# Packed attention and a gated convolution on one core: keys and queries turned by VectorE, scores in 32x32 tiles, the convolution moved to TensorE

## The chip, the cores and the metric

The kernel runs on one core of a Trainium2 chip. The metric is the device time of one execution in microseconds (us); lower is better. The kernel before took 320.68 us, the median of three runs (319.39 to 321.31). The core has TensorE (PE: matmuls and the transposes that go through its array; PEld is its weight load), VectorE (DVE), ScalarE (ACT), GpSimd (POOL) and SyncE (SP), which issues all DMA transfers here. Matmul results land in PSUM, which has eight banks of 512 f32 columns on 128 partitions.

## The reference

There are 8 batches, 8 heads, 576 tokens, 64 features a head and 32 packed rows `p` a head. The first attention lets the packed rows look at the tokens; the second lets the tokens look at the packed result. Its output, laid side by side over the heads (`x`, 576 x 512 a batch), goes through a causal convolution of five taps for each feature, a sigmoid, and two 512 x 512 weights:

```python
p_packed = softmax(p @ k^T / 8) @ v            # 32 x 64 for each head
x = softmax(q @ p_packed^T / 8) @ p_packed     # 576 x 64 for each head
gate_pre = sum(conv_w[j] * shift(x, 4 - j) for j in range(5))
out = (sigmoid(gate_pre) * (x @ w_val)) @ w_out
```

Everything is f32; the three weights arrive in double precision, and the kernel rebuilds f32 values from their 32-bit words.

## The kernel before, in words

All work of a batch is cut into streams with a letter each: loads `K`, `V`, `Q`, `P`; `k` and `q` (turning keys and queries so that the features lie on the partitions), `a` (first attention), `p` (turning the packed result), `s` (second scores and their exponentials), `t` (the normalised weights, split in a high and a low part), `w` (packed result times `w_val`), `x` (the attention output itself), `g` (convolution and gate), `v` (value product times gate), `o` (output product), and for the weights `L`, `W`, `C`, `O`. The string `ORDER` is a list of steps (`a1.2`: two steps of stream `a` of batch 1) written out ahead of the run. `InOrder` (line 82) makes each engine issue its instructions exactly in the order in which `ORDER` makes them. An instruction that waits therefore holds up all that stand behind it on its engine. The bar in `ORDER` closes the pool in which the raw weights lie, and opens the one for `gvh` and `gvl`.

What the steps do, for each batch:

- `load` (line 191) brings k, v and q as two tiles each of 96 partitions, four heads to a tile.
- `transposed` (line 296) turns one tile by 12 PE transposes of 96 x 96 into a PSUM bank, in three groups of four, and ACT copies each group to `kT` or `qT`. So k and q take 48 transposes and 12 copies a batch.
- `scores` (line 309) makes 8 matmuls for four heads, each with 64 contraction rows and 32 output partitions, 288 columns: the eight 64 x 32 tiles of the array. A batch has two for the first attention and two for the second.
- `attn_pack` (line 334) takes maximum (DVE), exponential (ACT), turns the weights by 6 PE transposes for each four heads (`at`, `a1t`), and multiplies by v (`pv`, 24 matmuls of 96 x 32).
- `attn_out` (line 384) turns the second scores by DVE's 32 x 32 transpose (`t2`), takes the maximum over 32 (DVE), subtracts it (POOL), takes the exponential (ACT); `weighted` sums (DVE), multiplies by the reciprocal (POOL), turns back (DVE, `a2`) and splits into `a2h` (ACT) and `a2l` (DVE).
- `mixed` (line 451) computes x itself: four groups of four matmuls with tiles of 32 x 64 (`x`), copied by ACT to `xp`.
- `gate` (line 483) makes the convolution from `xp`: one ACT multiplication and four DVE multiply-adds for each of four chunks of 128 features, then a tanh on ACT that stands for the sigmoid.
- `value` (line 503) makes 4 chunks of 12 matmuls (three products of high and low parts); DVE multiplies by the gate, ACT and DVE split the result into `gvh` and `gvl`.
- `project` (line 556) makes the output in 9 chunks of 128 tokens for each two batches, 12 matmuls of 512 columns a chunk (`o`).

PSUM is cut into two buffers of two banks (`big`), three of one bank (`mid`) and one of one bank (`out`) for the output product.

A product in f32 shows in the profile as two MATMUL records and one in fp32r, or a PE transpose, as one.

Of the kernel before, what the change touches and what calls it, by code (L numbers as in the profile page):

```python
# [45 lines left out]
ORDER = """
x0 L0.5 P0 W0.2 K0 W0 K0 W0 Q0 W0 P1 W0.3 V0 L0 W0 V0 Q0 W0.5 C0 L0 k0 W0 k0 P2 C0 W0 C0 W0 k0 C0 W0 C0 k0.4 K1
W0 C0 L0 k0.2 W0 k0.2 C0 W0 a0 k0 C0 W0 k0 a0 k0 K1 q0 W0 a0.2 W0 k1 q0.2 a0 k1 P3 q0.2 a0.3 L0 a0.2 Q1 a0 q0
a0.3 O0 V1 a0.7 O0 a0 O0 a0 O0.2 a0 p0 V1 O0.2 p0 O0 s0 O0 q0 w0 s0 q0 O0 s0 q0 O0 w0 s0 O0 w0 s0 q0.2 Q1 O0 t0
k1 q0 s0 k1 O0 k1 t0 s0 k1.2 K2 O0 k1 a1 t0 O0.2 s0 t0 x0 a1 O0 s0 k1 t0 a1 O0 k1.2 s0 k1.2 K2 t0 x0.2 k1 k2 P4  # L50
O0 x0 a1 O0 t0 g0 a1 q1 O0 g0 x0 a1.3 k2 g0 q1.2 a1.2 t0 q1.2 a1.2 g0 Q2 t0 x0 a1 O0 a1 q1 g0 x0.2 O0 a1 V2 g0
t0 v0 x0 O0 a1 g0 O0.2 a1 g0 q1 a1.2 O0 v0 a1.2 O0 a1 q1 g0 a1 O0.3 k2 O0 a1 p1 V2 k2.2 p1 q1 k2.2 q1 s1 g0 k2
K3 k2 O0 a2 k2 s1 k2 O0 q1 k2 a2 k2 O0.2 Q2 w1 s1 K3 q1 O0 g0 q2 s1 a2 g0 w1 O0 s1.3 w1 k2 k3 P5 O0 g0 q2.2 s1
a2 q2 x1 g0 q2 s1 | v0 a2 k3 Q3 q2 k3 v0 a2 v0 k3 s1 a2 g0 k3 a2 t1 q2 k3 a2.2 q2.2 a2 g0 a2 t1 q2 k3 v0 a2.2 k3
K4 g0 v0 k3 q2 a2 V3 k3.2 t1 Q3 g0 a2.2 g0 x1 v0 t1 g0 v0 q2 x1 t1 a2 t1 k3 x1 a2 k3 g0 t1 a2.2 x1 K4 v0 a2.2 k3
g0 v0 k4 V3 a2 a3 P6 p2 t1 p2 a3 t1 s2 v0 a3 q3 g0 q3 v0 s2 g0 x1 t1 g1 x1 v0 g1 v0 a3 x1 s2 k4 x1 g1 s2 a3 q3
k4 x1 g1 a3 q3.2 Q4 a3 w2 g1 s2 q3 v0 o0 g1 t2 g1 w2 g1 t2 k4 w2 v1 o0 g1 o0 t2 o0 g1 t2 v1 g1 v1 t2 s2 g1 x2.2
v1 g1 o0 g1 q3 a3 k4 x2 o0 s2 o0 a3 q3 g1 k4 s2 g1 s2 v1 g1 o0.2 s2 o0 v1 g1.2 t2 v1 g1 t2 a3 v1 o0 v1 a3 o0 x2
g1 a3 k4 t2 a3.2 k4 K5 v1 x2 q3 g1 a3 k4 V4 v1 a3.3 g1 k4 q3 v1.2 x2 g1 a3 q3 g2 v1 k4 a3 Q4 x2 q3 g2 v1 a3 g2
a3.2 x2 v1 x2 k4 V4 a3 g2 k4 t2 o1 K5 k4 t2 x2 g2.3 v2 o1 g2 o1 g2 a4 v2 p3 o1 p3 a4 v2 g2 a4 v2 g2 s3 o1 x3 w3  # L60
g2 o1 s3 g2 q4 s3 v2 w3 g2 s3 q4 w3 q4 o1 q4 v2 s3 g2 v2 t3 s3 o1 g2 t3 a4 o1 s3 q4 k5 o1 a4 q4 Q5 k5 g2 P7 a4.2
g2 s3 g2 t3 s3 a4 o1 k5 g2 x3 a4 o1 s3 a4 o1 t3 v2 a4 g2 x3 k5 t3 g2 v2 t3 o1.2 g2 t3 x3 v2 g2 a4 k5 a4.2 v2 t3
k5.2 v2 a4 v2 V5 k5 K6 a4 t3 x3.2 t3 a4 k5 g3 v2 x3 a4 k5 g3 k5 v2 a4 q4 g3 a4 q4 v2 o2 k5 x3 g3.2 a4 g3 x3 a4
g3 a4 x3 g3 q4 v3 V5 a4 q4 g3 o2 g3 o2.2 v3 g3 v3.2 g3 x4 g3 p4 q4 o2 g3 k5 p4 Q5 a5 k5 g3 o2 s4 q4 K6 o2 a5 s4
a5 g3 s4 g3 s4 a5 o2 w4 g3 o2 a5 g3 q5 a5.3 g3 o2 a5 g3 s4 w4 g3 q5 t4 a5 o2 s4 w4 a5 t4 k6 o2 a5 q5 k6 a5 s4 a5
q5 t4 v3 a5 V6 s4 t4 g3 s4 x4 v3 g3 q5 t4 k6 v3 Q6 s4 v3.2 q5 k6 t4 k6 x4 q5 k6.2 v3 q5 x4 t4 K7 k6 a5 v3 a5 q5
k6 t4 x4.2 q5 v3.2 t4 g4 t4 x4 a5 g4 k6 a5 k6 a5 v3 a5 x4 q5 g4 a5 x4 Q6 q5 v3 g4 k6 v3 o3 x4 g4.3 a5 o3 g4 k6
a5 a6 V6 k6 g4 o3 k7 p5 g4 o3 p5 K7 a6 g4 a6 g4 x5 a6 g4 s5 o3 g4 k7.2 o3 a6 q6 k7.2 g4 q6 o3 a6.2 s5 k7 g4 s5
v4 o3 g4 s5 o3 g4 q6 g4 v4 a6 w5 s5 g4 q6 a6 s5 t5 v4 a6 q6 w5 o3 g4 t5 Q7 q6 s5 a6 g4 q6 s5 o3 a6 k7 q6 g4 s5
o3.2 a6 k7 t5 g4 w5 t5 s5 t5 x5 o3 v4 k7 o3 t5 v4 x5 k7 t5 k7 v4 x5 k7 t5 v4 a6 x5.2 v4 x5 a6 V7 a6 g5 a6 v4 a6  # L70
g5 t5 x5 g5 a6 q6 v4 a6.2 x5 q6 g5 a6 v4 a6 t5 x5 q6 g5 a6 a7 V7 q6 Q7 v4 p6 g5 v4 a7 g5 p6 g5 a7 k7 v4 s6 k7 g5
v4 a7 q7 s6 q7.2 g5 w6 q7 v4 o4 g5 w6 a7 x6 g5 s6 a7.2 s6 w6 g5 v5 o4 g5 s6 o4 g5 s6 q7 v5 a7 o4 q7 g5 a7 v5 s6
v5 s6 v5 t6 o4 s6 o4 g5 q7 a7 o4 t6 q7 a7 s6 v5 g5 v5 t6 g5 v5.2 t6 g5 o4 t6 o4 x6 t6 a7 q7 a7 o4 x6 g5 t6 q7 v5
g5 v5 x6 o4 t6 q7 o4 v5.2 t6 g5 x6 q7 t6 x6 g5 x6 g6 v5 a7 x6 g6 x6 v5 g6 a7 x6 a7.2 v5 o5 a7 g6.2 v6 o5 g6 o5
g6 a7 o5 v6 a7 g6 v6 g6 v6.2 g6 o5.2 g6 a7 o5 g6 x7 g6 v6 a7 g6 v6 g6 a7 o5 v6 o5 g6 v6 a7 g6 p7 g6 o5 g6 v6 p7
g6 v6 g6 s7 v6 o5 v6 g6 o5 s7 g6 o5 s7 g6 s7 v6.2 w7 s7 v6 o5 t7 s7 o5 o6 w7 s7 t7 w7 t7 s7 o6 x7 t7 o6 s7 o6 t7
x7 s7 t7 x7 o6 t7 o6.2 x7.2 t7 g7 t7 g7 t7 v7 o6 g7 o6 g7 x7 g7 o6 g7.2 v7 x7 g7 v7 x7 g7 o6 v7.2 o6 x7 g7.2 o7
g7.2 v7 g7 v7 g7 v7.2 o7 g7.4 v7 g7 v7.3 o7 g7.3 o7 g7 v7.3 o7.15
# [28 lines left out]
def packed_attention_gated_conv(  # L107
# [24 lines left out]

    nc = tc.nc  # L140
# [50 lines left out]
    def load(b, nm, src, order):
        for g in range(G):
            m = st[nm, b, g] = tile_of(f"{nm}m", [TP, 4, NA, 2 * D], F32, f"{nm}m_{b}_{g}")
            sp.dma_start(m, src[b, 4 * g : 4 * g + 4].rearrange(order, a=NA, c=2))
# [451 lines left out]
```

## Time and profile before

| what | value |
|---|---|
| time, median of three runs | 320.68 us |
| time, lowest and highest of the runs | 319.39 and 321.31 us |
| span of the profiled execution | 317.6 us |
| PE busy | 284.6 us (90%) |
| DVE busy | 255.0 us (80%) |
| ACT busy | 212.7 us (67%) |
| POOL busy | 67.8 us (21%) |
| bytes read and written in HBM | 33.57 and 9.44 MB |

The profile gives the span, from the first to the last instruction, of one execution; its own time outside of the span isn't given. The median of the runs is 3.1 us above that span, and this is taken as what lies around it. Almost every instruction is issued from one helper, so the profile puts nearly all at line 90, and a group is told from another by the tiles it names: `kT<-kpt` is the copy of turned keys out of PSUM, `sig<-xp,cw,sig` is one tap of the convolution. `x8` is a count of instructions. "Idle before" is the time that the engine had nothing to do ahead of the group, and behind the arrow stands what ended it.

### The profile page before, as it was taken

What the parts mean: (1) busy time and instruction counts of PE and PEld (TensorE: products, weight loads), DVE (VectorE), ACT (ScalarE), POOL (GpSimd) and SP (SyncE); (2) the same over time, 40 slices, a digit from 0 to 9 for tenths busy, and PEclk for the clock granted to TensorE, in tenths of its full rate; (3) what the DMA queues carried; (4) which work ended last, traced back from release to release, by engine and by line L of the source; (5) the groups of instructions that cost most, each with busy time, mean ns of one, the idle gap of its engine ahead of it and who ended that gap; (6) DMA issues with size and microseconds to landing.
All of it is one profiled execution on the core that took longest, in us unless ns stands there. A gap on an engine that the chain in (4) does not pass through costs nothing.

```text
span 317.6 us, 7342 instructions
## 1 busy us (share of the span) xinstructions
PE 284.6 (90%) x2996; PEld 209.2 (66%) x2996; DVE 255.0 (80%) x396; ACT 212.7 (67%) x432; POOL 67.8 (21%) x71
## 2 busy tenths in 40 slices
PE   0088786879989999999999999999999999999993
PEld 0065243747557787677786876777688788667882
DVE  0983388679999997999789986897998977878771
ACT  2247669889876768666877787777856846556422
POOL 1312572464121220132002410231023000140000
PEclk9999758899999999999999999999999999999999
DMA  7999999999973239533657558243702011111005
GB/s 165 216 219 254 262 240 223 217 229 188 233 150 107 68 102 238 138 95 97 151 128 196 166 135 199 85 116 103 152 33 66 35 42 60 54 70 45 33 0 166
DMA packets 42475, 43.48 MB, mean 137 GB/s; under 512 B 6085, under 2 KB 36805, under 8 KB 42442
## 3 DMA queue, kind: packets, MB, share of 16 engines
q1 hardware_dynamic: 42442, 43.02, 58.1%
q8 instruction: 23, 0.38, 0.6%
q14 instruction: 10, 0.08, 0.1%
HBM read 33.57 MB, written 9.44 MB: 135 GB/s over the span
## 4 chain that ended last, share of the span: by engine, by line
PE 81%; ACT 8%; DMA 5%; DVE 3%; SPq 1%; issue 1%; ACTq 0%; DVEq 0%
PE o L90 32%; PE val L90 16%; PE x L90 6%; PE s L90 6%; PE kpt L90 5%; PE qpt L90 5%; PE pv L90 3%; DMA km<-in_k_dram 3%; PE at L90 3%; PE wp L90 3%; DMA wv_words<-in_moe_w_val_dram 2%; DVE sig L90 1%; ACT a1t L90 1%; ACT a L90 1%; ACT wo_top L90 1%; SPq L90 1%
## 5 line engine op out<-in xcount | busy, mean ns | idle before, releaser
L90 DVE SCALAR_TENSOR_TENSOR sig<-xp,cw,sig 128x576 f32<-128x576 f32 x128 | 106.4, 832 | 10.8 <-ACT sig L90 9.4
L90 PE MATMUL o<-woh,gvh 128*128 128x512 f32 x144 | 59.1, 411 | 0.1
L90 PE MATMUL o<-woh,gvl 128*128 128x512 f32 x144 | 56.5, 393 | 0.0
L90 PE MATMUL o<-wol,gvh 128*128 128x512 f32 x144 | 56.4, 392 | 0.0
L90 PE MATMUL val<-a2h,wph 128*128 128x288 f32 x128 | 39.4, 308 | 0.1
L90 ACT COPY osb<-o 128x512 f32<-128x512 f32 x34 | 19.8, 584 | 27.2 <-PE o L90 18.0
L90 PE MATMUL val<-a2h,wpl 128*128 128x288 f32 x128 | 37.9, 296 | 0.0
L90 PE MATMUL val<-a2l,wph 128*128 128x288 f32 x128 | 37.7, 295 | 0.0
L90 ACT ACTIVATE sig<-sig 128x576 f32<-128x576 f32 x32 | 22.0, 688 | 18.1 <-DVE sig L90 18.0
L90 POOL TENSOR_TENSOR t<-t,mx 128x576 f32<-128x576 f32 x16 | 23.1, 1442 | 47.8 <-DVE mx L90 46.6
L90 PEld LDWEIGHTS o<-woh,gvh 128*128 128x128 f32 x144 | 27.1, 188 | 9.4 <-issue 3.0
L90 POOL TENSOR_TENSOR t<-t,rs 128x576 f32<-128x576 f32 x16 | 22.0, 1372 | 50.1 <-DVE rs L90 44.6
L90 DVE SCALAR_TENSOR_TENSOR sig<-sig,val 128x576 f32<-128x576 f32 x32 | 23.9, 748 | 10.7 <-ACT sig L90 5.4
L90 PEld LDWEIGHTS o<-woh,gvl 128*128 128x128 f32 x144 | 27.1, 188 | 6.5 <-DVE gvl L90 0.4
L90 PEld LDWEIGHTS o<-wol,gvh 128*128 128x128 f32 x144 | 27.2, 189 | 4.6
L90 ACT COPY kT<-kpt 128x384 f32<-128x384 f32 x48 | 23.3, 485 | 10.2 <-PE kpt L90 10.0
L90 PE MATMUL kpt<-ident,km 96*128 96x96 f32 x192 | 26.8, 275 | 2.5 <-DMA km<-in_k_dram 2.4
L90 PE MATMUL qpt<-ident,qm 96*128 96x96 f32 x192 | 25.7, 262 | 3.2 <-ACT pT L90 1.9
L90 PEld LDWEIGHTS qpt<-ident,qm 96*128 96x128 f32 x192 | 19.6, 147 | 13.2 <-issue 7.5
L90 ACT COPY qT<-qpt 128x384 f32<-128x384 f32 x48 | 22.9, 485 | 6.9 <-PE qpt L90 6.9
L90 DVE TENSOR_TENSOR gvl<-sig,gvh 128x576 fp32r<-128x576 f32 x32 | 25.2, 788 | 2.6 <-ACT gvh L90 2.4
L90 PEld LDWEIGHTS kpt<-ident,km 96*128 96x128 f32 x192 | 21.0, 157 | 9.2 <-issue 4.9
(77 smaller groups left out, 515.1 us busy)
## 6 DMA issues: line engine op xcount, KB each, us to landing
km<-in_k_dram SPq DMA_DIRECT2D x16, 576.0 KB, 8.2
qm<-in_q_dram SPq DMA_DIRECT2D x16, 576.0 KB, 6.7
vm<-in_v_dram SPq DMA_DIRECT2D x16, 576.0 KB, 6.7
out_dram<-osb SPq DMA_DIRECT2D x24, 256.0 KB, 2.0
wv_words<-in_moe_w_val_dram SPq DMA_DIRECT2D x8, 256.0 KB, 6.1
wo_words<-in_moe_w_out_dram SPq DMA_DIRECT2D x4, 512.0 KB, 11.0
out_dram<-osb SPq DMA_DIRECT2D x8, 192.0 KB, 2.3
p<-in_p_dram SPq DMA_DIRECT2D x16, 64.0 KB, 8.4
```

What stands on the lines that cost most here:

```text
L90: made = getattr(self.engine, op)(*args, **kw)
```

## The change

Kernel after differs in the following parts.

- k, q and v come as two tiles each of 128 partitions (`m`, nine buffers for all three). A partition holds nine tokens in a row, 2304 bytes of each of two heads. A head now lies on 64 partitions, the even heads on the lower half and the odd ones on the upper, and these halves are the two groups g.
- k, q and p are turned by one DVE instruction for each tile, in blocks of 32 x 32, into `xT` and `pT`. PE transposes and ACT copies of k and q are gone. The 64 features now lie in two blocks of 32 (`c`), one behind the other.
- The scores of a whole batch are one product into four banks (`quad`): for each of the two feature blocks 16 matmuls of 32 x 32, 288 columns, the second block added to the first in PSUM. Matmuls for a batch and attention go from 16 to 32.
- The weights of the first attention are turned by 9 full PE transposes a batch, and `pv` has 72 matmuls of 64 x 32 a batch. A DVE multiplication by the reciprocal takes the place of two on ACT.
- The attention output x isn't computed any more. POOL multiplies the packed result by each of the five taps (`taps`, stream `c`, into `ppk`), and the convolution is 5 x 8 matmuls of 32 x 64 for each half of the tokens, added in `quad`, on `a2` read at five offsets. `mixed`, its ACT copies, ACT's first tap and DVE's four are gone; the tanh reads PSUM.
- For this, `a2` has a margin of four zeros and stays in two fixed tiles, and its tokens are written with a step of nine elements.
- The tap weights are spread over partitions by 10 small matmuls with a selection matrix (`sel`) at the start.
- PSUM is now one `quad` of four banks, one `big` of two and two `mid` of one bank. The output product uses `mid`.
- `ORDER` is another list.

```diff
-PSB = {'big': 2, 'mid': 3, 'out': 1}
+PSB = {"quad": 1, "big": 1, "mid": 2}
...
-            for a in range(NA):
-                pt = one(f"{nm}pt_{b}_{g}_{a}")[:, : 4 * TP].rearrange("x (j i) -> x j i", j=4)
-                for j in range(4):
-                    pe.transpose(pt[:, j], m[:, j, a], ident[:TP, :TP])
-                yield
-                act.copy(xT[:, :, TP * a : TP * a + TP], pt)
-                yield
+            dve.transpose(
+                xT.rearrange("a h e c z -> a (h e c z)"),
+                st[nm, b, n].rearrange("a h e d -> a (h e d)"),
+            )
+            yield
...
+        for c in range(2):
+            for t in range(NQ):
+                rows = slice(NP * t, NP * t + NP)
+                for hl in range(4):
+                    pe.matmul(
+                        s[heads[hl], t].rearrange("a (e z) -> a e z", z=NP),
+                        pT(rows, c, hl),
+                        st[f"{nm}T", b, hl // 2][rows, hl % 2, :, c, :],
+                        start=(c == 0),
+                        stop=(c == 1),
+                    )
...
+            pool.tensor_tensor(
+                ppk[:, g],
+                st["ppd", b][:, g].unsqueeze(1).broadcast_to([P, NT, D]),
+                cwb[:, g],
+                op=ALU.mult,
+            )
...
+            dve.transpose(
+                a2g.rearrange("a (t z e) -> a t e z", t=2, e=NE),
+                t2.rearrange("a (t e) z -> a t e z", t=2),
+            )
...
+        for half, hc in enumerate(halves):
+            x = quad(f"gate_{b}_{half}")
+            for kk in range(NT):
+                for hl in range(4):
+                    for g in range(G):
+                        pe.matmul(
+                            x[D * g : D * g + D, hl, :HS],
+                            ppk[heads[hl], g, kk],
+                            a2[heads[hl], g, hc.start + kk : hc.stop + kk],
+                            start=(kk == 0),
+                            stop=(kk == NT - 1),
+                        )
+            yield
+            sig = st["sig", b, half] = tile_of("sig", [P, NC, HS], F32, f"sig_{b}_{half}")
+            act.activation(sig, x[:, :, :HS], AF.Tanh, scale=0.5)
```

On PE, what stands ahead of the first output product changes. Before, 25 of the 48 groups of key transposes, 21 of the 48 of query transposes, 13 of the 32 scores products, 18 pairs of `at` transposes, 6 `pv`, 3 `wp`, 8 `x` and 4 value chunks. After, 4 of the 16 scores products (each of a whole batch now), 6 groups of three `at` transposes, 2 `pv`, 1 `wp`, 2 halves of the gate (batch 0) and 3 value chunks.

The loads at the start. SP before, from its first transfer on (`km`, `qm`, `vm` are tiles of k, q and v; the number behind is the buffer):

```order
L90 DMA wv_words<-in_moe_w_val_dram 64x1024 x8
L90 DMA cw_words<-in_moe_conv_w_dram 5x1024
L90 DMA p_94<-in_p_dram 128x2x64 x2
L90 DMA km_0_100<-in_k_dram 96x4x384
L90 DMA km_1_103<-in_k_dram 96x4x384
L90 DMA qm_0_106<-in_q_dram 96x12x128
```

SP after, from its first transfer on:

```order
L57 DMA cw_words<-in_moe_conv_w_dram 40x128
L57 DMA wv_words<-in_moe_w_val_dram 128x1024
L57 DMA p_86<-in_p_dram 32x4x64 x4
L57 DMA km_0_93<-in_k_dram 128x2x576
L57 DMA wv_words<-in_moe_w_val_dram 128x1024
L57 DMA km_1_101<-in_k_dram 128x2x576
```

The first keys move ahead of three of the four pieces of `w_val`.

DVE at the second attention of batch 2, where the weights for the convolution are made. Before (`t` is the turned scores, `mx`, `sm` and `rs` maximum, sum and reciprocal, `a` the weights turned back; the taps of the convolution stand between):

```order
L90 STREAM_TRANSPOSE t_2_1146<-s_2_0_1148 128x576
L90 TENSOR_TENSOR a2l_941<-a_1_939,a2h_940 128x576
L90 SCALAR_TENSOR_TENSOR sig_3_1036<-sig_3_1036,val_3_1169 128x576
L90 SCALAR_TENSOR_TENSOR sig_0_1187<-xp_0_876,cw,sig_0_1187 128x576
L90 TENSOR_REDUCE mx_2_1147<-t_2_1146 128x18
```

DVE after, at the same batch:

```order
L57 STREAM_TRANSPOSE t_2_0_1362<-s_2_1329 128x576
L57 STREAM_TRANSPOSE t_2_1_1364<-s_2_1329 128x576
L57 TENSOR_REDUCE mx_2_0_1385<-t_2_0_1362 128x18
L57 SCALAR_TENSOR_TENSOR sig_1_1219<-sig_1_1219,val_1_2_1372 128x576
L57 TENSOR_REDUCE mx_2_1_1409<-t_2_1_1364 128x18
L57 TENSOR_REDUCE sm_2_0_1411<-t_2_0_1362 128x18
L57 TENSOR_TENSOR sm_2_0_1411<-sm_2_0_1411,eps 128x18
L57 RECIPROCAL sm_2_0_1411<-sm_2_0_1411 128x18
L57 TENSOR_TENSOR gvl<-sig_1_1219,gvh 128x2x288
L57 STREAM_TRANSPOSE a_0_75<-t_2_0_1362 128x2x9x32
```

Both halves of the scores are now turned at once, straight out of the one product, and the taps between are gone.

POOL at batches 1 and 2. Before (`mx` and `rs` as above, `xp` the margin for the convolution):

```order
L90 MEMSET xp_0_876 128x4x2
L90 TENSOR_TENSOR t_1_751<-t_1_751,mx_1_752 128x576
L90 TENSOR_TENSOR t_1_751<-t_1_751,rs_1_938 128x576 x2
L90 MEMSET xp_1_1184 128x4x2
L90 TENSOR_TENSOR t_2_1146<-t_2_1146,mx_2_1147 128x576
L90 TENSOR_TENSOR t_2_1146<-t_2_1146,rs_2_1274 128x576
```

POOL after, at batch 2 (`ppk` is the packed result times the taps, `t2_2_0` and `t2_2_1` the two halves):

```order
L57 TENSOR_TENSOR t2_2_0_1362<-t2_2_0_1362,mx2_2_0_1385 128x576
L57 TENSOR_TENSOR t2_2_0_1362<-t2_2_0_1362,sm2_2_0_1411 128x576
L57 TENSOR_TENSOR t2_2_1_1364<-t2_2_1_1364,mx2_2_1_1409 128x576
L57 TENSOR_TENSOR ppk_2_1435<-ppd_2_1138,cwb_74 128x320 x2
L57 TENSOR_TENSOR t2_2_1_1364<-t2_2_1_1364,sm2_2_1_1446 128x576
```

The four steps of POOL still stand one behind the other, and the two tap products stand among them.

More of the change, by code (lines that the diff above doesn't have):

```diff
@@ L49 @@
[L49 to L58, printed above, removed]
@@ L74 @@
[L74 to L78, printed above, removed]
+NB = {
+    "words": 5, "m": 9, "xT": 4, "pT": 1, "a1t": 1, "pp3": 1, "ppk": 1, "t2": 3, "a2h": 3, "a2l": 3,
+    "wp": 3, "sig": 3,
+}
@@ L189, in load_p, with load @@
         yield
[L191 to L194, printed above, removed]
+    def load(b, nm, src):
+        rows = src[b].rearrange("h s d -> (h s d)").rearrange("(h a x) -> a h x", h=4, a=P)
+        for n in range(2):
+            m = st[nm, b, n] = tile_of("m", [P, 2, NE, D], F32, f"{nm}m_{b}_{n}")
+            sp.dma_start(m.rearrange("a h e d -> a h (e d)"), rows[:, 2 * n : 2 * n + 2])
@@ L272, in conv_weights @@
         yield
-        cps = one("cwps")
-        for c in range(NC):
-            pe.transpose(cps[:, c * 8 : c * 8 + NT], top[:, c * P : c * P + P], ident[:NT, :NT])
+        cps = big("cwps")[:, :, : NT * D].rearrange("a g (k d) -> a g k d", k=NT)
+        for g in range(G):
+            for kk in range(NT):
+                pe.matmul(
+                    cps[:, g, kk],
+                    sel[:, g, kk].rearrange("a h j -> a (h j)"),
+                    top,
+                    start=True,
+                    stop=True,
+                )
         yield
-        dve.tensor_copy(cw, cps[:, : 8 * NC].rearrange("a (c e) -> a c e", e=8)[:, :, :NT])
+        act.copy(cwb, cps)
         yield
@@ new lines, in attn_pack @@
+            yield
+        dve.tensor_scalar_add(rs, rs, 1e-9)
+        dve.reciprocal(rs, rs)
+        yield
+        a1t = tile_of("a1t", [P, NE, P], F32, f"a1t_{b}")
+        for part in range(3):
+            es = slice(part * 3, part * 3 + 3)
+            at = one(f"at_{b}_{part}")[:, : 3 * P].rearrange("a (e y) -> a e y", y=P)
+            for e in range(3):
+                pe.transpose(
+                    at[:, e], a1[:, es.start + e].rearrange("a g t z -> a (g t z)"), ident
+                )
+            yield
+            act.copy(a1t[:, es], at)
+            yield
@@ new lines, in attn_pack @@
+        pv = big(f"pv_{b}")[:, :, :D]
+        for e in range(NE):
+            for g in range(G):
+                rows = slice(D * g, D * g + D)
+                for hl in range(4):
+                    pe.matmul(
+                        pv[heads[hl], g],
+                        a1t[rows, e, heads[hl]],
+                        st["v", b, hl // 2][rows, hl % 2, e, :],
+                        start=(e == 0),
+                        stop=(e == NE - 1),
+                    )
+        yield
@@ new lines, in attn_pack, with packed_turned @@
+        ppd = st["ppd", b] = tile_of("ppd", [P, G, D], F32, f"ppd_{b}")
+        dve.tensor_tensor(ppd, pv, rs.unsqueeze(2).broadcast_to([P, G, D]), op=ALU.mult)
+        yield
+    def packed_turned(b):
+        ppd = st["ppd", b]
+        pp3 = tile_of("pp3", [P, 2, G, 2, NP], F32, f"pp3_{b}")
+        for c in range(2):
+            act.copy(
+                pp3[:, c],
+                ppd[:, :, NP * c : NP * c + NP].unsqueeze(2).broadcast_to([P, G, 2, NP]),
+            )
+            yield
+        pt = one(f"ppTt_{b}")[:, : 3 * P].rearrange("a (c y) -> a c y", y=P)
+        for c in range(2):
+            pe.transpose(pt[:, c], pp3[:, c].rearrange("a g t z -> a (g t z)"), ident)
+        pe.transpose(pt[:, 2], ppd.rearrange("a g d -> a (g d)"), ident)
+        yield
+        ppT = st["ppT", b] = tile_of("ppT", [P, 3, P], F32, f"ppT_{b}")
+        act.copy(ppT, pt)
+        yield
@@ new lines, in value @@
+        for half, hc in enumerate(halves):
+            for c2 in range(0, NC, 2):
+                chunks = slice(c2, c2 + 2)
+                vps = big(f"val_{b}_{half}_{c2}")
+                for c in range(2):
+                    cols = slice((c2 + c) * P, (c2 + c + 1) * P)
+                    n = 0
+                    for g in range(G):
+                        ah, al = st["ah", b, g], st["al", b, g]
+                        for w, x in ((wph, ah), (wpl, ah), (wph, al)):
+                            pe.matmul(
+                                vps[:, c, :HS], w[:, g, cols], x[:, hc], start=(n == 0), stop=(n == 5)
+                            )
+                            n += 1
+                yield
+                gv = st["sig", b, half][:, chunks]
+                dve.scalar_tensor_tensor(
+                    gv, gv, 1.0, vps[:, :, :HS], op0=ALU.add, op1=ALU.mult
+                )
+                yield
+                hi, lo = (
+                    x[:, chunks, base + hc.start : base + hc.stop] for x in (gvh, gvl)
+                )
+                act.copy(hi, gv)
+                yield
+                dve.tensor_tensor(lo, gv, hi.bitcast(F32), op=ALU.subtract)
+                yield
@@ L560, in project @@
         if b == B - 1:
-            accs = {c: one(f"o_{b}_{c}") for c in range(4, 7)}
-            accs[7] = one(f"o_{b}_7", "out")
+            last = quad(f"o_{b}")
+            accs = {c: last[:, c - 4] for c in range(4, 8)}
+            accs[8] = one(f"o_{b}_8")
             for n4 in range(NC - 1):
@@ L565, in project @@
                     product(accs[c], c, n4)
-                yield
-            accs[8] = big(f"o_{b}_8")[:, 0]
-            for n4 in range(NC - 1):
-                product(accs[8], 8, n4)
-            yield
+                    yield
         for c in chunks:
```

407 lines of the change are left out of this document (141 added, 266 removed).

## Prediction, made before the changed kernel ran

> **What bounds the kernel now.** I read the page first, then the chain of waits in order of time, then the busy times by stretch, then PE's timeline in a steady stretch. From the page: PE's busy time, PE's tenths in 40 slices of 7.94 us, the GB/s in the same slices, and the chain that ended last, by engine and by group.
>
> ```profile
> PE 284.6 (90%) x2996; PEld 209.2 (66%) x2996; DVE 255.0 (80%) x396; ACT 212.7 (67%) x432; POOL 67.8 (21%) x71
> PE   0088786879989999999999999999999999999993
> GB/s 165 216 219 254 262 240 223 217 229 188 233 150 107 68 102 238 138 95 97 151 128 196 166 135 199 85 116 103 152 33 66 35 42 60 54 70 45 33 0 166
> PE 81%; ACT 8%; DMA 5%; DVE 3%; SPq 1%; issue 1%; ACTq 0%; DVEq 0%
> PE o L90 32%; PE val L90 16%; PE x L90 6%; PE s L90 6%; PE kpt L90 5%; PE qpt L90 5%; PE pv L90 3%; DMA km<-in_k_dram 3%; PE at L90 3%; PE wp L90 3%; DMA wv_words<-in_moe_w_val_dram 2%; DVE sig L90 1%; ACT a1t L90 1%; ACT a L90 1%; ACT wo_top L90 1%; SPq L90 1%
> ```
>
> PE holds 81% of the chain. The chain in order of time (start, length) shows where it takes over: the first output product begins at 95.55 us, and PE ends with output products at 312.4.
>
> ```profile
> 95.55 2.94 PE o L90 x12
> ...
> 303.84 8.54 PE o L90 x36
> 312.40 0.58 ACT osb L90
> ```
>
> The stretches of 20 us (length, then PE, PEld, DVE, ACT, POOL busy) say the same: PE is full from 100 us on; ahead of that nothing is, and DVE has 11.79 + 8.94 + 15.63 + 17.31 = 53.7 us of work in the first 80 us, 67%.
>
> ```profile
> 0.00:20.00 20.00, 3.54 (x19) 2.91 (x20) 11.79 (x17) 6.24 (x10) 5.00 (x11) 1.00 0.96 196
> 20.00:40.00 20.00, 16.86 (x218) 9.41 (x216) 8.94 (x20) 12.97 (x31) 6.00 (x5) 0.91 1.13 251
> 40.00:60.00 20.00, 16.53 (x188) 9.95 (x188) 15.63 (x30) 15.88 (x35) 8.77 (x8) 0.74 1.15 227
> 60.00:80.00 20.00, 16.89 (x280) 11.85 (x279) 17.31 (x26) 18.53 (x45) 11.61 (x9) 1.00 1.05 210
> ...
> 100.00:120.00 20.00, 20.00 (x195) 16.11 (x194) 18.93 (x29) 13.29 (x27) 3.39 (x4) 1.00 0.31 92
> ```
>
> So the span is 95.6 us of head, 216.9 us of PE without a break (95.55 to 312.40), and 5.2 us of tail (312.4 to 317.6: the last copy and transfer). The median of the runs is 3.1 us above the span. A change counts by PE's work and by how early the output products can begin; work taken off DVE and ACT counts only in the head.
>
> **PE's work, part by part.** PE's timeline in a full stretch (start, length as recorded). Matmuls overlap in the records, so I price a group by the distance from its start to the next start.
>
> ```profile
> 157.46 0.38 PE L90 MATMUL at<-ident,a 128*96 128x128 f32 x2
> 157.77 0.71 PE L90 MATMUL x<-a,ppd 32*64 32x288 f32 x8
> 158.42 0.88 PE L90 MATMUL pv<-vm,a1t 96*32 96x64 f32 x48
> 159.22 0.55 PE L90 MATMUL qpt<-ident,qm 96*128 96x96 f32 x4
> 159.56 0.38 PE L90 MATMUL val<-a2h,wph 128*128 128x288 f32 x1
> ...
> 161.24 0.40 PE L90 MATMUL o<-woh,gvh 128*128 128x512 f32 x1
> ...
> 164.02 0.38 PE L90 MATMUL ppTt<-ident,ppd 128*128 128x128 f32 x2
> 164.23 0.49 PE L90 MATMUL qpt<-ident,qm 96*128 96x96 f32 x4
> 164.56 0.49 PE L90 MATMUL kpt<-ident,km 96*128 96x96 f32 x4
> 164.99 0.72 PE L90 MATMUL s<-kT,pT 64*32 64x288 f32 x16
> 165.50 0.69 PE L90 MATMUL s<-qT,ppT 64*32 64x288 f32 x16
> 166.12 0.50 PE L90 MATMUL o<-woh,gvh 128*128 128x512 f32 x1
> ...
> 169.61 1.06 PE L90 MATMUL wp<-wv,ppT 64*32 64x512 f32 x16
> 170.61 0.55 PE L90 MATMUL qpt<-ident,qm 96*128 96x96 f32 x4
> ```
>
> Prices: two `at` 0.31, `x` 0.65, `pv` 0.80, four key or query transposes 0.33 to 0.43 (I take 0.37), a value chunk 1.68, an output chunk 2.78, two turns of the packed result 0.21, a scores product 0.51 or 0.62 (0.57), `wp` 1.00.
>
> Removed: 96 groups of transposes x 0.37 = 35.5; 32 `x` x 0.65 = 20.8; 32 scores x 0.57 = 18.2; 48 `at` x 0.31 = 14.9; 16 `pv` x 0.80 = 12.8; 16 pairs of turns x 0.21 = 3.4. Together 105.6 us.
>
> Added:
> - Scores. The eight tiles of one product take 0.51 us for two passes when the next has the same shape, so 0.25 a pass of 288 columns, and some 0.1 for a change of shape. A new product has two feature blocks of two passes: 4 x 0.25 + 0.1 = 1.1, if 16 tiles run as eight do. 16 x 1.1 = 17.6. If only eight run at once: 8 x 0.25 + 0.1 = 2.1, 33.6. I take the first, since the matmuls of the second product stand in the array 0.51 behind the first with nothing lost.
> - Gate. `x` has two passes of 288 columns in 0.65, four tiles of 32 x 64. A half of the gate has five taps of two passes, eight such tiles each: 10 x 0.25 + 0.15 = 2.65, and 16 x 2.65 = 42.4. With four tiles at once, 5.15: 82.4. I take the first, again by the scores' row, where four column groups read four streams of data at once; the gate needs two.
> - `pv`: 12 passes of 64 columns take 0.80 - 0.14, so 0.055 each; now 18 passes, 1.15 a batch, 9.2. If it is the 16.7 ns a matmul (0.80 / 48) that counts, 144 of them take 2.4, 19.2. I take the first; the 0.055 fits a pass of 64 columns as 0.25 fits 288.
> - 24 groups of three full `at` at 0.46, 11.0; 24 turns of the packed result, 2.5; the tap weights once, some 1.5.
>
> Together 84.2. PE's work falls by 105.6 - 84.2 = 21.4 us. Output, value and `wp` products are unchanged.
>
> [...]
>
> **When the output products begin.** The other engines' rows (mean ns behind the comma):
>
> ```profile
> L90 DVE SCALAR_TENSOR_TENSOR sig<-xp,cw,sig 128x576 f32<-128x576 f32 x128 | 106.4, 832 | 10.8 <-ACT sig L90 9.4
> L90 DVE STREAM_TRANSPOSE t<-s 128x576 f32<-128x576 f32 x16 | 12.4, 772 | 5.4 <-PE s L90 5.3
> L90 DVE TENSOR_REDUCE sm<-t 128x18 f32<-128x576 f32 x16 | 11.9, 746 | 0.7 <-ACT t L90 0.5
> L90 DVE SCALAR_TENSOR_TENSOR wv_top<-wv_top,wv_words 128x512 uint32<-128x512 uint32 x4 | 4.6, 1155 | 0.3
> L90 POOL TENSOR_TENSOR t<-t,mx 128x576 f32<-128x576 f32 x16 | 23.1, 1442 | 47.8 <-DVE mx L90 46.6
> L90 POOL TENSOR_TENSOR t<-t,rs 128x576 f32<-128x576 f32 x16 | 22.0, 1372 | 50.1 <-DVE rs L90 44.6
> L90 ACT ACTIVATE t<-t 128x576 f32<-128x576 f32 x16 | 11.1, 692 | 0.5 <-POOL t L90 0.5
> L90 ACT CAST wph<-wp 128x1024 fp32r<-128x1024 f32 x8 | 8.1, 1013 | 2.5 <-PE wp L90 2.5
> L90 ACT COPY kT<-kpt 128x384 f32<-128x384 f32 x48 | 23.3, 485 | 10.2 <-PE kpt L90 10.0
> km<-in_k_dram SPq DMA_DIRECT2D x16, 576.0 KB, 8.2
> wo_words<-in_moe_w_out_dram SPq DMA_DIRECT2D x4, 512.0 KB, 11.0
> ```
>
> DVE loses 106.4 us of taps and gets 32 turns of 128 x 1152. The nearest row is 0.77 us for half the size; twice that is 1.54, and I take 1.4: 45 us. So DVE falls from 255 to some 195 us. ACT loses 23.3 us of key copies, about as much for q, and the copies and first taps around x; POOL gets 16 tap products of 320 columns, 0.8 us each by its 1442 ns for 576. None of these becomes the bound; DVE stands at two thirds of the span.
>
> Loads: the first output product stands behind the keys of batch 2 on PE. What is loaded ahead: eight weight pieces of 512 KB, twelve tiles of 576 KB (k of three batches, q of one, v of two), p: 11.5 MB. Before's slices add up to 10.8 MB at 47.6 us and 12.5 MB at 55.6, so the keys land near 51 us. Two turns, a scores product and a value chunk follow: 57 us.
>
> DVE: ahead of the gate's low part that the first output chunk reads stand 9 turns of k and q (12.6), 3 of p (1.2), the weights' steps (some 16), 19 steps of 576 columns at about 0.77 (14.6), and 2 to 3 us of small ones: 47 us. At the 67% of before that is done at 70 us. I take 62, since its waits are for loads that now come earlier, and keep 56 to 72.
>
> PE's work in the head was 46 x 0.37 + 13 x 0.57 + 18 x 0.31 + 6 x 0.80 + 3 x 1.00 + 8 x 0.65 + 4 x 1.68 + 8 x 0.21 = 51.4 us. Now 4 x 1.1 + 6 x 0.46 + 2 x 1.15 + 1.00 + 2 x 2.65 + 3 x 1.68 + 0.6 + 1.5 = 22.9. Behind the first output product remain 216.9 + 51.4 - 21.4 - 22.9 = 224.0 us.
>
> New waits. The chain from a batch's second scores to its gate: two turns 1.54, maximum 0.75, subtraction 1.44, exponential 0.69, sum 0.75 and small steps 0.5, multiplication 1.37; then POOL takes the second half: 1.44, 0.69, 1.25, 1.37; then a turn 0.77. That is 12.6 us, and some dozen handovers. In batches 1 to 3 PE has in between two `at` groups, a value chunk, three output chunks, `wp` and `pv`: 0.9 + 1.7 + 8.3 + 1.0 + 1.2 = 13.1. So PE waits at the gate for a microsecond or so, and everything behind it in its order waits too; from batch 4 on more stands in between. I add 4 us, with bounds of 0 and 20. The turn back with a step of nine elements is priced at 0.77; at twice that it lengthens this chain by less than 2 us.
>
> The sum: 62 + 224 + 4 + 5.2 = 295.2 us of span, and 3.1 around it: 298 us.
>
> **The rivals.**
> - PE waits for PSUM. There is one `quad` and one `big`. A batch needs `quad` for both scores and both gate halves: by the rows 3.4 (product, two maxima, an exponential) + 2.6 + 2 x (2.65 + 1.14 for a tanh of 1152 by the 1013 ns of 1024) = 13.6 us of some 30 a batch. For it: before had six buffers for what is now four. Against it: half the time is free, and other products stand between in PE's order. With half a microsecond lost at each of some 30 of these products, 15 us more: 313.
> - The head is bound by loads alone, and no wait is added: 56 + 224 + 5.2 + 3.1 = 288, and with rows of 2304 bytes for the earlier smaller ones, as low as 283. Against it: DVE's 47 us.
> - Slower: tiles of four row groups do not run eight or sixteen at a time. The trace shows `x` with four tiles and scores with eight, never more. At those numbers the gate costs 40 us more and the scores 16: 354. The same comes if weight loads of 64 columns stand in line: `x` has eight in 0.65 us, at most 81 ns each, and 80 of them make 6.5 us for a half of the gate, 62 us more: 360. It decides from an added 22 us on, over half of this. For it: no row has more than eight tiles. Against it: the eight tiles lost nothing.
> - The head is not shortened (DVE and the order keep it near 80 us): 316.
>
> [...]
>
> **How the numbers follow.** The forecast has 0.57, the waits for PSUM 0.17, the early one 0.11, the slow tiles 0.09, the long head 0.06. A change under 0.5% (1.6 us) can't be told here. Faster holds all but the slow tiles and a part of the worst of the waits: 0.87; same 0.03; slower 0.10. The range goes from the early case to the PSUM case, 283 to 315, and leaves out the slow tiles and a part of the long head.
>
> **What would show it.** In the changed kernel's profile: the first `o` at 56 to 72 us; a gate half about 2.65 us and a scores product about 1.1 on PE's timeline; PE without a break behind the first `o`, some 225 us; DVE near 195 us busy. It is wrong if a gate half takes 4 us or more, if PE's waits for `sig`, `t` or `a` add up to over 20 us, or if the first `o` comes after 80 us.

## The result, and the profile after

The changed kernel takes 333.85 us, the median of four runs (333.23 to 334.83), against 320.03 us of the kernel before beside it (318.75 to 321.31): a ratio of 1.045, 95% interval 1.040 to 1.051. It is slower by 4.5%. The forecast was 298 us, in a range of 283 to 315.

From the page of the changed kernel, the lines that answer to those shown of before: busy times, PE's tenths and the granted clock in 40 slices of 8.29 us, GB/s, and the chain that ended last.

```profile
PE 283.1 (85%) x4516; PEld 208.6 (63%) x4516; DVE 204.5 (62%) x294; ACT 133.8 (40%) x238; POOL 82.7 (25%) x80
PE   5357659599869998998599989979989999999975
PEclk9999999879979999999979999997999999999999
GB/s 217 404 345 312 154 3 11 319 47 215 138 333 36 140 166 92 110 95 216 397 13 36 243 5 328 56 176 34 107 4 32 65 34 33 65 34 46 19 62 128
PE 61%; DVE 12%; issue 6%; ACT 6%; POOL 1%; DVEq 0%; ACTq 0%
```

DVE, ACT and the loads did about what was forecast: DVE fell from 255.0 to 204.5 us, and the first 20 us of loads run far faster (320 GB/s for 196). PE did not become free. Its busy time is as before, its matmul records went from 2996 to 4516, and "issue" now holds 6% of the chain: time in which PE waited for nothing that the profile shows. The chain of waits around the first output product and around the end:

```profile
67.16 3.18 PE val L57 x12
70.34 2.91 PE o L57 x12
...
323.32 4.47 PE o L57 x18
327.80 0.02 issue
327.82 0.58 ACT osb L57
```

PE's timeline has the first `o` itself, which overlaps the matmul ahead of it:

```profile
70.14 0.54 PE L57 MATMUL o<-woh,gvh 128*128 128x512 f32 x1
```

The output products begin at 70.1 us (62 was taken, with 56 to 72 kept) and PE ends at 327.8. So 257.6 us lie behind the first `o`, where 228.0 were forecast. PE's waits in that stretch (who waits, for what: us in total, times, longest):

```profile
PE gate L57 <- issue: 6.9, 2, 3.5
PE pv L57 <- issue: 4.8, 3, 2.3
PE ppTt L57 <- ACT pp L57: 3.3, 1, 3.3
PE pv L57 <- DVE wpl L57: 2.7, 3, 1.0
...
PE gate L57 <- ACT sig L57: 0.5, 2, 0.3
PE gate L57 <- DVE a L57: 0.2, 1, 0.2
```

The wait for `pp` lies ahead of the first `o`. Behind it, the waits with a name in the program are small; the largest are five without one, 11.7 us. PE's timeline shows one (start, length, and in brackets the idle time and what ended it):

```profile
157.26 1.66 PE L57 MATMUL pv<-vm,a1t 64*32 64x64 f32 x144 [1.04 <-DVE wpl L57]
158.85 2.17 PE L57 MATMUL gate<-a,ppk 32*64 32x288 f32 x57
164.40 1.20 PE L57 MATMUL gate<-a,ppk 32*64 32x288 f32 x23 [3.38 <-issue]
```

PE stops in the middle of a gate half, with its data ready, and goes on 3.38 us later. The DMA view of that time names what was missing. First the transfers from 154 to 161.8 us, then from 161.8 to 165 (queue, kind: packets, MB, share of the 16 engines):

```profile
q1 hardware_dynamic: 1345, 2.84, 101.3%
```

```profile
q1 hardware_dynamic: 574, 1.25, 103.1%
q8 instruction: 1, 0.02, 2.1%
```

Queue q8 brings instructions in pieces of 16 KB, and their number goes with PE's: there are 35 of them, and 23 in the kernel before; PE has 9032 instructions here (each matmul record has its weight load) and had 5992, and an experiment below with 6984 has 27 pieces. So they are taken to be PE's, and a piece holds some 260. In the 7.8 us of the first view, in which PE used up a `pv` and most of a gate half, no piece came, while the data queue filled the DMA engines (101%). The piece came at 161.85, took 1.07, and PE went on 1.5 us after it landed. By the records behind these rows, all five stops are alike in one thing: PE ran dry 457 to 535 instructions after the piece before had begun. In three (at 90.62, 161.02 and 221.02, of 3.5, 3.4 and 2.3 us) the DMA engines had been busy with data for three to seven microseconds, and the next piece began 1.2 us after, 0.8 us after, and just as PE ran dry. In the two others (192.48 and 240.97, of 1.3 and 1.2 us) the DMA engines were nearly free (a share of 0.06 and less in the microsecond before the piece and during it), and the piece had begun 1.2 us ahead; its own length of 0.9 to 1.0 us and the 1.4 us that follow outlasted that.

The stop is paid for twice. The stretches around it (start:end, length, busy times, then the granted clock, DMA share and GB/s):

```profile
161.00:164.40 3.40, 0.02 (x4) 0.00 (x1) 0.00 (x0) 0.00 (x0) 0.00 (x0) 1.00 1.05 397
164.40:166.10 1.70, 1.70 (x27) 1.15 (x27) 0.00 (x0) 0.45 (x1) 0.00 (x0) 0.98 0.93 340
166.10:169.50 3.40, 3.40 (x29) 2.85 (x35) 0.67 (x1) 0.87 (x2) 0.00 (x0) 0.51 0.03 12
```

Then, 1.6 us after PE went on, it runs at half the clock for 3.4 us: some 1.7 us more. It is the same behind the stops at 90.62 and 221.02; behind the wait for `pp` the half clock lasts 6.8 us.

The stretch behind the first `o`, by groups from start to next start, in us. The two columns on the right are experiments told below.

| term | forecast | after | loads once (e7) | both orders (e8) |
|---|---|---|---|---|
| first `o` | 62 | 70.1 | 69.9 | 65.1 |
| 12 scores products | 13.2 | 18.4 | 18.4 | 18.4 |
| 6 `pv` | 6.9 | 14.9 | 13.8 | 12.0 |
| 14 gate halves | 37.1 | 47.8 | 39.6 | 40.6 |
| 36 output chunks | 100.1 | 104.7 | 104.8 | 104.2 |
| 29 value chunks | 48.7 | 49.4 | 48.5 | 48.6 |
| `at`, `wp`, turns | 18.0 | 17.0 | 17.2 | 18.0 |
| idle with a named releaser | 4.0 | 5.6 | 6.0 | 6.4 |
| tail | 5.2 | 3.6 | 3.6 | 3.7 |
| span | 295.2 | 331.4 | 321.7 | 317.0 |

A wait that falls inside a group counts with the group, so the stops without a name lie inside `pv` and gate. The forecast's row of `at`, `wp` and turns is what its 224.0 leaves beside the others. The rows show two kinds of error: undisturbed groups cost more than priced (`pv` and scores), and gate and `pv` hold stops that weren't in the sum at all.

### The profile page after: what moved, and what is told of

Its sections match the earlier page's. It is cut to its first block, busy times and chain, and to the rows that moved or that the text cites. A ratio compares the mean times of both kernels' runs of the same rounds, so it can differ in the third digit from the quotient of the medians.

```text
span 331.4 us, 10048 instructions
## 1 busy us (share of the span) xinstructions
PE 283.1 (85%) x4516; PEld 208.6 (63%) x4516; DVE 204.5 (62%) x294; ACT 133.8 (40%) x238; POOL 82.7 (25%) x80
## 4 chain that ended last, share of the span: by engine, by line
PE 61%; DVE 12%; issue 6%; ACT 6%; POOL 1%; DVEq 0%; ACTq 0%
PE o L57 23%; PE val L57 15%; PE gate L57 11%; PE s L57 6%; PE pv L57 3%; PE at L57 2%; DVE a L57 2%; DVE gvl L57 1%; DVE sm L57 1%; DVE wpl L57 1%; DVE wo_top L57 1%; ACT osb L57 1%; ACT sig L57 1%; DVE a2l L57 1%; PE ppTt L57 1%
## 5 line engine op out<-in xcount | busy, mean ns | idle before, releaser
L57 PE MATMUL gate<-a,ppk 32*64 32x288 f32 x1280 | 47.3, 419 | 7.9 <-issue 6.9
L57 POOL TENSOR_TENSOR t<-t,mx 128x576 f32<-128x576 f32 x16 | 20.8, 1303 | 99.3 <-DVE mx L57 99.3
L57 PEld LDWEIGHTS gate<-a,ppk 32*64 32x64 f32 x1280 | 28.3, 135 | 24.3 <-issue 13.0
L57 POOL TENSOR_TENSOR t<-t,sm 128x576 f32<-128x576 f32 x16 | 19.2, 1199 | 53.5 <-DVE sm L57 46.2
L57 ACT CAST gvh<-sig 128x576 fp32r<-128x576 f32 x32 | 21.6, 674 | 25.5 <-DVE sig L57 22.9
L57 PEld LDWEIGHTS val<-a2h,wph 128*128 128x128 f32 x128 | 24.8, 194 | 10.3 <-issue 6.1
L57 ACT ACTIVATE sig<-gate 128x1152 f32<-128x1152 f32 x16 | 18.1, 1131 | 31.8 <-PE gate L57 31.8
L57 PEld LDWEIGHTS val<-a2h,wpl 128*128 128x128 f32 x128 | 25.1, 196 | 0.4
L57 PEld LDWEIGHTS val<-a2l,wph 128*128 128x128 f32 x128 | 25.1, 196 | 0.0
L57 PE MATMUL s<-kT,pT 32*32 32x288 f32 x512 | 18.1, 513 | 7.9 <-DVE kT L57 7.9
```

What stands on the lines that cost most here:

```text
L57: made = getattr(self.engine, op)(*args, **kw)
```

## The experiments

The main theory was the supply of instructions: runs of small matmuls use PE's instructions up faster than the pieces come. Its rivals were the single `quad` and `big` in PSUM with DVE's order, and, for the supply itself, two causes: the mere rate, or pieces held up behind data.

**Small matmuls spread (e1_spread).** In batches 1 to 6 an output chunk goes between `pv` and the gate, or between the scores and `pv`, and `wpl` earlier. One place of the list:

```diff
-t1 w1 a2 t1 s1 o0.2 t1.2 w1 t1 P5 t1 w1 k4 o0 t1 o0 q2 o0 a2 g1
+t1 w1 a2 w1.2 t1 s1 o0.2 t1.3 P5 t1 k4 o0 t1 o0 q2 a2 o0 g1
```

> The same instructions as in the changed kernel, in another order: in batches 1 to 6 an output chunk of large matmuls stands between the product pv and the gate, or between the scores and pv, so that no more than about 160 small matmuls stand in a run. Supply theory (PE is held up by the supply of its own instructions where small matmuls stand together): the five gaps put down to issue behind the first output product, 11.7 us in all, fall to under 4 us, the stretches at a granted clock of 0.5 behind them go, and the time is 316 to 322 us. Rival (one quad and one big in PSUM, and waits for DVE): the gaps return under the names of DVE or ACT, and the time stays at 331 to 335 us.

It took 324.27 us (ratio to before 1.012, 1.008 to 1.016). In batch 5 the new list moved only a store, so `pv` still stood right behind the scores there. PE's waits behind 60 us:

```profile
PE ppTt L57 <- ACT pp L57: 5.9, 2, 3.3
PE gate L57 <- DVE a L57: 2.2, 3, 1.1
PE pv L57 <- issue: 2.0, 2, 1.4
```

The gaps by issue fell to 2.0 us, 1.4 of them in batch 5, and the granted clock dips only in the head and after PE's last matmul. The same instructions in another order are 8.9 us faster by the span (322.5 for 331.4). The time is 2 us above the range expected, for new waits for `pp` (2.6) and `a` (2.0); and 2.7 of the gain is the wait for `wpl`, which went too. So the run speaks for supply, but it changed DVE's and ACT's order with it.

**Where the pieces are held up (e3_one_v, e7_loads_once).** First the loads of v were left out from batch 1 on, then those of k, v and q:

```diff
+        if b > 0:
+            for n in range(2):
+                st[nm, b, n] = st[nm, 0, n]
+                yield
+            return
```

> The values v are loaded for batch 0 only and used for all batches (fourteen loads of 576 KB are left out). If the pieces of PE's instructions come late because they stand behind bursts of data loads, the issue gaps behind the first output product fall from 11.7 to under 6 us and the time is 322 to 329 us. If the gaps are set by how fast PE uses its instructions up, they stay at 10 to 13 us and the time at 331 to 335 us.

It took 330.3 us (1.028, 1.022 to 1.035), between the two expectations; the gaps fell from 11.7 to 8.4. The stop near 221 fell to 0.7 us; of the two in the gate one stood (3.5) and one was 1.8, with k and q still filling the DMA engines there. That run settled nothing by itself.

> Keys, values and queries are loaded for batch 0 only and used for all batches (all later loads of 576 KB are left out), nothing else is changed. If PE's pieces of 16 KB come late because they stand behind data in busy DMA engines, the issue gaps behind the first output product fall from 11.7 to under 3 us, the halved clock behind them goes, and the time is 318 to 326 us. If the gaps are set only by how fast PE uses instructions up, they stay at 9 to 12 us and the time at 328 to 334 us.

It took 321.89 us (1.008, 1.004 to 1.012): 9.7 us less span than the changed kernel (321.7), with every PE and DVE instruction in its place. By the medians it is 12.0 us faster; the span is that of one execution. Its waits, its transfers from 148 to 157 us, and the gate half that had stopped for 3.38 us:

```profile
PE pv L57 <- issue: 3.6, 3, 1.3
PE pv L57 <- DVE wpl L57: 2.7, 3, 1.0
...
PE gate L57 <- issue: 0.9, 2, 0.7
```

```profile
q1 hardware_dynamic: 288, 0.52, 15.1%
q8 instruction: 1, 0.02, 0.7%
```

```profile
154.05 2.18 PE L57 MATMUL gate<-a,ppk 32*64 32x288 f32 x59
156.42 1.19 PE L57 MATMUL gate<-a,ppk 32*64 32x288 f32 x21 [0.20 <-issue]
```

The gaps fell to 4.5 us, not under 3 as expected; the time is as expected. So of 11.7 us, 7.2 came from pieces that stood behind data. The three stretches of half clock behind the stops went too (some 1.7 us each), one new one came near the end (at 312.4), and the stretch behind the first `o` got 9.4 us shorter (257.6 to 248.2). The pieces themselves show it as well, since both kernels have the same list of instructions. Counted in PE's recorded instructions, the pieces of the three stops with busy DMA engines began at the 2228th, 4525th and 6566th, and in e7 at the 2138th, 4422nd and 6406th; those of the two others at the 5371st and 7142nd, and in e7 at the 5373rd and 7124th. The 4.5 us that stay, at 1.1 to 1.3 us where `pv` follows other small matmuls and 0.9 in the gate, come with hardly any load running: that is the rate. In the kernel before, with 23 pieces, none of PE's waits is by issue. By what rule the DMA engines choose between a piece and data, no run here shows.

**PE's own work taken away (e2_pv_ninth).**

```diff
-        for e in range(NE):
+        for e in range(1):
```

> The product pv of the first attention takes only the first of its nine blocks of tokens (eight ninths of the product with v are left out, 1024 matmul records fewer). Supply theory: pv loses 13 us of its own time (14.9 to about 2) and with it go most of the issue gaps (10 us or so of 11.7) and some of the clock's dips: 304 to 312 us. Rival (PSUM and DVE waits): only its own time goes, and part of that turns into waits for DVE: 320 to 326 us.

It took 316.14 us (0.985, 0.978 to 0.992), between the two. Not one gap by issue is left behind the first `o`, as the supply theory has it. But the 13.2 us of `pv` that went had 4.8 of the gaps in them already, which I counted twice, and waits for `a`, `sig` and `pp` grew by some 4 us together. The rival is right that far: with the supply mended, the in-order waits for DVE and ACT come next.

**The cost put into the kernel before (e4_before_pv3).**

```diff
-            for a in range(NA):
+            for a in (0, 1, 2) * 3:
```

> The kernel before with each product pv made three times over (same result, 288 matmul records in a group instead of 96; 3072 records more in all). Supply theory: a group takes about 288 x 8.3 ns = 2.4 us and more instead of 0.80, so 16 x 1.6 = 26 us at least, and issue gaps appear that the kernel before does not have: 350 to 362 us. Without any limit of supply (0.055 us a pass as priced in the prediction): 16 x 1.3 = 21 us, 341 us, and no gaps.

The counts in that text take weight loads as well; by records a group goes from 48 to 144. It took 357.46 us (1.117, 1.110 to 1.124), as the supply theory had it, though not by its working. An undisturbed group takes 2.15 us from start to next start:

```profile
174.22 2.22 PE L90 MATMUL pv<-vm,a1t 96*32 96x64 f32 x144
176.37 0.55 PE L90 MATMUL kpt<-ident,km 96*128 96x96 f32 x4
```

That is 36 passes at the prediction's 0.055, and its 0.14, together 2.12: the passes set it, not a rate of instructions, since as many records take 1.59 us in the changed kernel's `pv`. Sixteen times 1.34 are 21.4 us. The other 15 are what is left for the gaps, 11.8 us, which the kernel before has not, and for the half clock in the head (37.5 us of it, for 13.7 in the kernel before):

```profile
PE pv L90 <- issue: 10.1, 3, 5.5
...
PE pTt L90 <- issue: 1.5, 1, 1.5
```

All but 0.2 us stand before 108 us, where loads are densest (every slice with over 200 GB/s lies there). Later a tripled group costs its passes and no more.

**What sets a group's length (e9_columns), one run.** On the kernel with loads for batch 0 only, each scores matmul was cut into 160 and 128 columns, and `pv` took half the columns of v:

```diff
+                for es in (slice(0, 5), slice(5, NE)):
...
-                        st["v", b, hl // 2][rows, hl % 2, e, :],
+                        st["v", b, hl // 2][rows, hl % 2, e, : D // 2],
```

> On the kernel with loads for batch 0 only, to see what sets the length of a group of small matmuls: pv takes only 32 of the 64 columns of v (the other half of its result is a copy), with the same number of matmuls; each matmul of the scores is cut in two of 160 and 128 columns, twice the matmuls for the same columns. If the rate of matmuls sets them (some 8 ns a record): an undisturbed pv stays at 1.4 to 1.6 us and a scores product rises from 1.53 to 2.0 or more. If the columns that stream set them: pv falls to about 0.9 and the scores stay at 1.5 to 1.6.

A scores product and a `pv` in it, next to those of the changed kernel below:

```profile
103.35 2.42 PE L57 MATMUL s<-kT,pT 32*32 32x160 f32 x128
105.70 0.40 PE L57 MATMUL val<-a2h,wph 128*128 128x288 f32 x1
...
126.75 1.42 PE L57 MATMUL pv<-vm,a1t 64*32 64x32 f32 x144 [0.90 <-DVE wpl L57]
128.10 1.81 PE L57 MATMUL gate<-a,ppk 32*64 32x288 f32 x40
```

```profile
104.48 1.60 PE L57 MATMUL s<-kT,pT 32*32 32x288 f32 x64
106.02 0.40 PE L57 MATMUL val<-a2h,wph 128*128 128x288 f32 x1
...
125.45 1.66 PE L57 MATMUL pv<-vm,a1t 64*32 64x64 f32 x144 [0.92 <-DVE wpl L57]
127.04 0.74 PE L57 MATMUL gate<-a,ppk 32*64 32x288 f32 x16
```

From start to next start, the same columns in twice the matmuls take 2.35 instead of 1.54 us, 12.7 ns for each record more; half the columns in the same matmuls take 1.35 instead of 1.59. So in these two groups the number of matmuls weighs more than their columns. `pv` came out a little below the 1.4 expected. The run took 345.62 us. It has 43 pieces for 35, and stops by issue of 7.8 us behind its head where e7, with as few loads, has 4.5: the rate again.

**The head (e5_head).** Two steps of ACT, the second copy into `pp` and the second tanh of batch 0, go ahead of the first `gvh`, which waits for the last raw weights:

```diff
-| p1 Q1 k2 v0.4 g0 Q1 p1.2 a2
+| p1.2 g0 Q1 k2 v0.4 Q1 p1 a2
```

> The changed kernel with two ACT steps moved at the head: the second copy of the packed result and the second tanh of batch 0 stand ahead of the first gvh instead of behind it, since gvh waits for the raw weights' pool to close at 62 us. If PE's start on the output products was held by ACT's order, PE's wait of 3.35 us for pp and the halved clock behind it go, the first output product comes at 64 to 66 us instead of 70.1, and the time is 326 to 330 us. If the weights themselves or DVE's key turns bind, it stays above 68 us and the time at 331 to 334.

It took 329.86 us (1.030, 1.023 to 1.038), and the first `o` came at 66.0: ACT's order had held PE, for 4.1 us of the 8.1 that the head was late. For the rest, the chain of waits shows `w_out`'s conversion over DVE, ACT and POOL, which ends at 62 us in both; no run took it away.

```profile
66.03 0.40 PE L57 MATMUL o<-woh,gvh 128*128 128x512 f32 x1
```

**Both together (e6_both, e8_best).** e6 joins e1 and e5, puts an output chunk ahead of `pv` and of the first gate half of batch 5, and moves batch 6's second `pp`. e8 moves two steps more; for the first half of batch 0 DVE takes both value chunks before the first `gvl`:

```diff
+                if b == half == 0:
+                    split.append((chunks, gv))
+                    if c2 == 0:
+                        continue
+                for ch, y in split if b == half == 0 else [(chunks, gv)]:
```

> The spread order with the head's two steps moved, an output chunk put ahead of pv in batch 5 and ahead of the first gate half of batch 5, and the second copy of the packed result of batch 6 moved ahead. Supply theory with the head's order: 324.3 less 5 for the head and 3 to 5 for a fetch gap, a wait for pp and a wait for DVE: 313 to 318 us, faster than the kernel before. If gaps only change their place: 321 to 325 us.

> The kernel with both orders changed, and two more steps moved: the copy of an output chunk on ACT in batch 6 goes ahead of steps that wait for DVE (PE waits 2.2 us for it), and for the first half of batch 0 DVE multiplies the second value chunk by the gate ahead of making the first gvl (PE waits 1.5 us for that). If these waits are PE's own and nothing else is late right behind them: 319.8 less 3 to 3.6, 315 to 317.5 us, faster than the kernel before by about 1%. If something else is late there, 318 to 320.

e6 took 319.76 us, the time of the kernel before (0.999, 0.995 to 1.004), 2 us above its range: a new wait of 2.2 for `osb` took the place of one removed. e8 took 318.86 (0.995, 0.992 to 0.998). It misses 315 to 317.5 as well. The wait for `sig` went from 1.8 to 0.4 and that for `osb` ahead of `at` went, but waits for `a` and `ppT` came behind it:

```profile
PE pv L57 <- issue: 2.1, 2, 1.5
PE gate L57 <- DVE a L57: 2.0, 2, 1.1
PE at L57 <- ACT a L57: 1.7, 1, 1.7
...
PE at L57 <- ACT ppT L57: 1.0, 1, 1.0
```

The same arithmetic as in the changed kernel, in another order, takes 14.4 us less span (317.0), and is half a per cent faster than the kernel before.

## Why the prediction was wrong

None of its own three signs of being wrong came up: an undisturbed gate half is under 4 us, the waits for `sig`, `t` and `a` add up to under 10 (8.0 of them for `a` in the head, under 1 behind the first `o`), and the first `o` came ahead of 80. What failed is what it expected beside them: PE without a break behind the first `o`, for some 225 us, and a scores product of about 1.1 us.

- **The step that failed** is "Behind the first output product remain ... 224.0 us", with 4 us for waits. It sums the prices of groups and lets PE run them without a break, since it did so before. 11.7 us of stops for instructions, and the half clock behind three of them, were no term of the sum and no rival. The counts that would have raised it were at hand: half as many matmuls again on PE, in runs of 224 and more, while loads came faster than before. Spread by e1 and freed of loads in e7, the stops fell to 2.0 and 4.5 us. Of the 36.2 us by which the span is longer than forecast (331.4 for 295.2), 11.7 are these stops, some 5 the half clock (an estimate: three times 1.7), 8.1 the head and 7.8 the price of scores and `pv`; the 3.5 left over are spread.
- **Scores and `pv`** were priced by passes that stream, 1.1 and 1.15 us; undisturbed they take 1.53 and 1.59. For 12 and 6 of them that is 5.2 and 2.6 us. The scores' 1.53 lies between the two prices considered, 1.1 for sixteen tiles at once and 2.1 for eight. For `pv` the prediction had another price in hand ("If it is the 16.7 ns a matmul (0.80 / 48) that counts", 2.4 us) and set it aside, as the passes explained the row too. Neither was right: e4 shows passes setting four-tile groups (2.15 us for 36), e9 shows the count of matmuls weighing more in `pv` and scores, with eight and sixteen (twice the scores' records take 2.35 us for 1.54). The row couldn't tell the two apart, so the range should have held both.
- **The gate** was right: 2.61 us for an undisturbed half, 2.65 forecast, the price for eight tiles at once. The slower side had been given to slow tiles, and the gate's were not slow. Slower came by another way.

```profile
100.15 2.61 PE gate L57 x80
```

- **Weight loads in a line**, the other ground for the slower side, would at 81 ns each have made a half of the gate 6.5 us. It takes 2.61 with its 80 loads, 33 ns for a load and its matmul, so at that price they don't stand in line; `pv` and the scores, with loads of 32 columns, have 11 ns for one (1.59 us, 144) and 24 (1.53 us, 64). No term of the sum hung on it.
- **Output chunks** take 2.88 us in the kernel before (103.5 for 36), not the 2.78 read from one row. The sum holds them within the measured 216.9 us, so the 3.4 us that the table's 100.1 lacks are no error of it by themselves. They answer to `at`, which was taken off at 0.31 a pair: 30 pairs behind the first `o` of the kernel before take 6.7 us, 0.22 each, so 2.6 us too much went off.
- **The head** stayed within its bounds, 70.1 in 56 to 72, but 8.1 above the value taken. e5 gives 4.1 of it to ACT's order.
- **Waits** had 4 us in the sum, for `a` at the gate, and the table has 5.6 behind the first `o`. That this is near is luck: the gate waits 0.2 us for `a`, and the rest are waits for a place in PSUM, the rival at 313 us, which took 15 for them: 2.7 in `pv` for `big`, 2.2 in the last output chunks, 0.5 for the tanh.
- **DVE** was forecast near 195 and has 204.5. The turns of k are as priced (1.35, for 1.4), but the turn with a step of nine takes 1.25, not 0.77: 7.7 us over sixteen. From the groups on DVE:

```profile
L57 DVE STREAM_TRANSPOSE kT<-km 128x1152 f32<-128x1152 f32 x16 | 21.1, 1349 | 0.0
L57 DVE STREAM_TRANSPOSE a<-t 128x576 f32<-128x576 f32 x16 | 20.0, 1252 | 3.1 <-POOL t L57 3.1
...
L57 DVE STREAM_TRANSPOSE t<-s 128x576 f32<-128x576 f32 x16 | 11.6, 758 | 11.9 <-PE s L57 11.9
```

What stays open: e8 runs 317.0 us of span where 295.2 were forecast. By the table, 3.1 of that is the head, and the rest lies behind the first `o`: scores 5.2, `pv` 5.1, output 4.1, gate 3.5, waits 2.4, less 1.6 in value chunks and tail. The gate takes 40.6 us there, for 14 times 2.61 (36.5): two halves stop for `a` after two of their 80 matmuls and take 4.2 and 4.4 us with the wait, and one takes 3.2. How to have `a` there in time was not tried.

## What to carry to other kernels

When a change trades few large matmuls for many small ones, count PE's instructions as a stream of its own: at some 260 to a piece of 16 KB, a run that uses several hundred in 4 us (a `pv` and a gate half here: 448) needs its pieces in time, and here they came late where data filled the DMA engines (101%). Put large matmuls between the runs, and keep bursts of loads away from them: here that took the stops from 11.7 us to 2.0 (e1) and 4.5 (e7). Price a group of small tiles by its count of matmuls as well as by its columns (12.7 ns for each record more in e9's scores), and where a row fits both, keep both ends.

## What the runs showed of the hardware

- PE's instructions come in 16 KB pieces over the DMA engines (0.9 to 1.5 us each in the changed kernel); with the DMA engines full of data two pieces began 0.8 and 1.2 us after PE had run dry, and PE went on 1.4 to 1.5 us after each landed.
- A stop of 2.3 us was followed by half the clock for 3.4 us, not with the stop but 0.8 us after its end (0.2 and 1.6 us after the two stops of 3.5 and 3.4):

```profile
221.10:223.30 2.20, 0.00 (x0) 0.00 (x0) 0.00 (x0) 0.59 (x2) 0.00 (x0) 1.00 0.00 0
...
224.10:227.50 3.40, 3.40 (x9) 2.66 (x10) 2.64 (x4) 1.53 (x4) 0.00 (x0) 0.50 0.02 5
```

  No length of rest decides it by itself: a wait of 2.6 us in e1 (at 218.8) was followed by no dip, and one of 1.9 us in the kernel before (it ends at 52.59) by one, 3.4 us at a granted clock of 0.50 from 53.80 on. What sets a dip off was not shown.
- Of DVE's 32 x 32 turns, the turn of `a`, 576 columns, takes 1.25 us where it writes with a step of nine elements, and 0.77 in the kernel before, where it writes in a row.
